# A new order table for a fused attention and maxout-FFN kernel: the same instructions, placed anew on the engines

## The chip, the cores and the metric

The kernel runs on one core of a Trainium2 chip. The metric is the device time of one execution in microseconds (us), as the median of several runs. A core has a tensor engine (PE, with its weight loads PEld), VectorE (DVE), ScalarE (ACT), GpSimd (POOL) and SyncE (SP). Each engine works through its own instructions strictly in order, and waits on semaphores for the others. Transfers between memory and the core are issued by SP (one DMA queue, q1 in the profile) or by POOL (another, q0) and are carried by 16 DMA engines, which both queues share.

## What is computed

```python
def phi(x):                       # x: [8, 8, 576, 64], w_phi: [64, 128]
    proj = einsum('bhsd,df->bhsf', x, w_phi)
    proj = proj - max(abs(proj), axis=-1, keepdims=True)
    return concatenate([exp(proj), exp(-proj)], axis=-1)
q_p, k_p = phi(q), phi(k)
kv  = einsum('bhsf,bhsd->bhfd', k_p, v)
num = einsum('bhsf,bhfd->bhsd', q_p, kv)
den = einsum('bhsf,bhf->bhs', q_p, sum(k_p, axis=2))[..., None] + 1e-06
x   = (num / den).transpose(0, 2, 1, 3).reshape(4608, 512)
h   = maximum(maximum(x @ w1, x @ w2), x @ w3)      # w1, w2, w3: [512, 768]
out = h @ w_out                                     # w_out: [768, 512]
```

Linear attention with a learned feature map, and behind it a feed-forward layer (FFN) that takes the maximum of three projections. All inputs and the output are 32-bit floats.

## The kernel before, in words

The attention is cut into 16 units (`attention(u)`, L429 on): unit u is half of the eight heads of batch u // 2, 18 tiles of 128 rows. A unit goes through these steps, each called a node:

- Loads. Units 0 to 3 have q and k loaded by POOL's queue, which turns them to bf16 on the way (L451, L466; k of unit 0 comes through SP, L458, and is cast, L462). Units 4 to 15 have them loaded by SP in 32 bits (`load`, L373 and L378) and cast by POOL (L510). The last 64 rows of each head of q, the tails, come in small pieces of 256 bytes through SP (L383), for two units at a time; units 0 to 3 have them cast by POOL (L487). v comes through SP (L373). For units 1 to 3 a one-element DVE copy (`gate`, L479) holds the load of v back until an earlier unit is transposed.
- Transposes of q and k: by PE (L495) with a DVE copy out (L500) for units 0 to 3, by a DMA transpose on SP (L514) for the others.
- Projections on PE (L536), two exponentials per group on ACT (L545), maxima of the absolute value on DVE (L548), the products of v with the exponential of the maxima (em, L558, on ACT) on POOL (`va`, L566).
- kv on PE (L587), the transposed projections and their exponentials (L607, L613), num and den on PE (L638), scaling, sum and quotient on DVE and POOL (L641, L644, L646, L648), and a transpose of the result into xT (PE L658, or a DMA on SP, L665).

The FFN uses max(x w1, x w2, x w3) = x w1 + max(0, x (w2 - w1), x (w3 - w1)). So w2 and w3 are replaced by their differences from w1 (L763): three pieces of w2 - w1 on POOL, three of w3 - w1 on DVE. The straight part x w1 w_out goes through a product of w1 and w_out that is computed once on the chip: w1 is transposed by PE (L775) and multiplied with w_out (L789). A chunk of 512 tokens (`chunk`, L671 on) takes for each of six columns an `up` group of four matmuls with w2 - w1 (L688), evacuated by ACT (L696) or DVE (L698), an `up2` group with w3 - w1 (L688 too), evacuated by DVE as a maximum (L694), then for each of four tiles the straight part (L716) and the down product (L721), an evacuation (L729) and a store through SP (L736). There are eight chunks, and a ninth for the tails of all batches, whose last tile is done in two halves of 256 columns: half i = 0 stores two pieces through SP, half i = 1 one through SP and one through ACT.

The four weights are loaded by POOL's queue, cast to bf16 on the way (L421): w1, w2 and w3 into w_bf, w_out into wout_bf.

What sets the order of it all is `PLAN`, a table of 1572 words made beforehand. A word such as `178S0@7.2` puts node 178 on SP (T is PE, D DVE, A ACT, G POOL, S SP), gives each of its buffers that is not placed yet a slot (0 here), and names a start time. `plan()` takes the nodes in the table's order, sets engine and slots, and emits them; each engine gets its instructions in that order. The start times serve only `fill()`, which may put idle matmuls into PE's gaps; it puts none here. The figures given with a node when it is built (costs, pipe, lat, packet, dmas) and the list of what it depends on are what a layout program would use. The replay doesn't read them. Waits follow from what the instructions read and write.

Of the kernel before, what the change touches and what calls it, by code (L numbers as in the profile page):

```python
# [89 lines left out]
401S0@12.2 44A0@12.2 98D@12.3 66A@12.4 46G0@12.5 69A@12.9 100D@13.0 108T112511@13.1 35A@13.2 38D@13.6 62A@13.6  # L90
113T31@13.8 256G@13.9 181G@14.1 70A@14.1 112D@14.2 45G@14.3 48A@14.4 103T40@14.6 109A@14.6 117D@14.8 257T2@14.9
104A@15.1 111D@15.4 261T3@15.6 61A@15.6 329S0@15.6 47G@15.7 49G@15.9 262D2@16.0 105A@16.1 107D@16.2 52T073@16.4
59A@16.5 106D@16.8 110A@17.0 50G@17.2 116D@17.4 60A@17.5 118T45@17.7 259T0@18.0 53A@18.0 122D@18.1 128A1@18.2
114A@18.4 123T67@18.5 51G@18.6 121D@18.7 400S@18.8 130G1@18.8 54A@18.9 152T411@18.9 115A@19.1 126D@19.4 154A@19.6
127D@19.7 55T31@19.7 124A@19.9 260D@20.0 119A@20.1 129G@20.1 182T6@20.4 56A@20.6 258D@20.7 125A@20.8 186T0@20.9
71A0@21.1 147T37@21.3 187D0@21.3 132A@21.3 57D@21.5 153A@21.5 72T20@21.6 135G@21.7 183D@21.7 120A@21.8 131G@21.9
75T14@22.0 133G@22.2 149A@22.3 73D0@22.3 184T5@22.4 76D@22.8 155A1@22.8 328S@22.9 151A@23.0 136T162@23.0 74D@23.2
148A@23.4 134G@23.5 77D@23.6 83T10@23.7 150A@23.9 138D@24.0 142T34@24.2 185D@24.2 137A@24.4 80T27@24.6 145A@24.6
78D0@24.8 139T65@25.0 84D1@25.1 143A@25.1 79G0@25.2 81D@25.5 146A@25.6 1187T1@25.7 85D@25.9 327S@26.0 144A@26.1
1185T2@26.3 82D@26.3 1188A0@26.6 406G1@26.6 141D@26.7 159T40@26.9 140D@27.0 86D1@27.2 156T37@27.2 160D0@27.5  # L100
1186A@27.5 87G@27.5 1183T5@27.6 157D@27.9 164T61@28.2 161D@28.3 1184A@28.5 223T4300@28.6 158D@28.7 88T2@28.9 404G@29.0
165D1@29.2 90T0@29.2 225A@29.4 403G@29.5 179D1@29.6 167T75@29.6 166D@29.7 1195T6@29.9 89A@29.9 405G@30.1 254D@30.1
168D@30.2 227A@30.5 162D0@30.7 334G2@30.7 91D@30.9 255S@31.0 224A@31.0 1189T21@31.2 163D1@31.4 226A@31.5 1196A@32.0
169D@32.1 1D@32.5 206T007000@32.6 197T4365@32.7 170D1@32.7 1190A@32.8 209D@33.0 172T1@33.3 171D@33.3 208A@33.5
1191T2@33.6 207A@33.9 201D@34.0 198A@34.2 180S@34.2 1179G@34.6 210D@34.7 199A@34.8 174T0@34.9 205D@35.0 1193T4@35.2
203A@35.3 200D@35.6 175A@35.8 173D@36.2 1192A@36.4 188T7630@36.6 1178G@36.7 1194A@36.9 228T1@37.0 1207T2@37.2
195D@37.3 230A@37.4 189A@37.7 196D@37.9 1209T4@38.1 229A@38.2 1208A1@38.4 204D@38.5 407G@38.8 1205T1@39.0 191D@39.1
202A@39.3 1177G@39.5 408S1@39.6 1181D@39.7 194A@39.7 1203T3@39.9 1210A@40.2 192D@40.3 1215T2@40.7 211A0@40.7
1182D@40.9 1204A@41.0 190A@41.5 1206D@41.5 331G@41.6 1217T5@41.6 193A@42.0 1216D@42.1 333G@42.2 272T11473611@42.6
212G0@42.7 1180D@42.8 218T10@43.0 277A@43.3 1219T2@43.3 280D@43.4 273A@43.8 276D@44.0 1221T3@44.2 222A@44.2 279D@44.6  # L110
219A@44.7 1201T4@45.1 1220D@45.2 274A@45.2 213G@45.2 220A@45.7 1218D@45.8 1213T2@45.9 1202A@46.2 1222D@46.4 278A@46.7
1199T1@46.8 275D@47.0 221A@47.2 1214D@47.6 214G@47.7 263T5436@47.8 332G@48.0 215T070@48.2 265A@48.5 271D@48.5
1200A@49.0 267D@49.1 281T23@49.4 268A@49.5 1211T1@49.6 285D@49.8 282A@50.0 270D@50.1 216A@50.2 1223T5@50.5 217A@50.6
1212D@50.8 231A0@50.9 269A@51.1 266D@51.4 243T27@51.4 544S0@51.7 240T01@51.7 284D@52.0 1224T@52.0 474S@52.3 244D0@52.3
286A1@52.5 283A@52.7 241D@52.8 287G1@52.8 335S0@52.9 264A@53.0 245D@53.2 235T62@53.3 242D@53.6 1225A0@53.6
293T3011@53.8 298T47@54.0 236D1@54.0 303T1@54.2 297A@54.2 1231T5@54.4 237D@54.6 304A@54.7 246D0@55.0 299A@55.0
232T62@55.3 288G@55.3 305A@55.5 1232T@55.6 301A@55.8 233D@55.9 300A@56.3 234D@56.4 302A@56.7 1227T1@56.9 238D1@57.0
296A@57.2 1233D1@57.2 294A@57.7 289G@57.8 247D0@57.9 409T00642700@57.9 480G0@58.1 290T105@58.3 295A@58.4 417D@58.6
479G@58.8 415A@58.8 412D@59.2 550G1@59.3 543S0@59.4 1228T@59.6 292A@59.8 416D@59.8 549G@60.0 473S@60.0 411A@60.1
291D@60.4 239G@60.6 306A1@60.6 475S@60.6 413D@60.8 414A@60.8 318T32@60.9 315T50@61.3 410A@61.3 319D0@61.5  # L120
366T7600@61.7 1229A2@61.8 545S0@61.9 316D@61.9 307T43@62.1 320D@62.4 369A@62.4 684S0@62.5 310T51@62.5 317D@62.8
368A@62.9 1235T2@62.9 547G@63.0 614S@63.1 308D1@63.2 370A@63.4 321D0@63.6 248T0@63.8 367A@63.8 311D@63.8 322G1@64.0
371T46@64.2 309D@64.3 249A@64.4 354T115711@64.5 330S1@64.5 1236T@64.7 312D@64.7 356A@65.0 313D1@65.3 374A@65.3
546G@65.4 314D@65.6 373A@65.7 325T3@66.0 478G@66.0 476S@66.0 375A@66.2 250T0@66.3 358D@66.4 323T1@66.6 477G@66.7
326D@66.7 251A@66.9 439T5611@67.0 324D@67.2 548G@67.2 441A@67.5 427T30@67.6 683S0@67.6 357D@67.7 690G2@67.7
1247T1@67.9 431D@68.0 355A@68.2 1237D3@68.4 440A@68.5 1241T3@68.7 372A@69.0 430D@69.0 615S@69.0 1248D0@69.3 442A@69.4
336T7524@69.7 428A@69.9 1239T1@70.2 429A@70.4 344D@70.4 1238S@70.6 443A@70.6 340D@71.0 1249T0@71.1 1242A@71.1
1226S@71.2 343D@71.6 1240A@71.6 402S@71.8 345T2673@72.1 339D@72.2 1250A@72.2 1245T1@72.6 347A@72.8 349D@72.8 613S@73.1
351A@73.3 348D@73.4 1261T0@73.5 687G@73.7 337A@73.8 352D@74.0 689G@74.3 1251T2@74.4 338A@74.4 1234S@74.6 353D@74.6
688G@74.8 359A0@74.9 346A@75.1 481S2@75.2 360G0@75.2 1253T5@75.2 1262D@75.3 1246A@75.6 1252D@75.9 362A@76.1  # L130
1259T7@76.1 342A@76.2 1254D@76.5 350A@76.7 418T6012@77.1 341A@77.2 376T3@77.5 361G@77.7 1243T5@77.7 425D@77.8
# [161 lines left out]
def kernel(  # L293
# [133 lines left out]
    def attention(u):  # L427
        un = units[u]
        b, ct0 = u // 2, (u % 2) * 2  # L429
        by_pe = u < BY_PE  # L430
# [15 lines left out]
        main_q, main_k, cast = [], [], {}  # L446
# [409 lines left out]
```

## Time and profile before

| | |
|---|---|
| median of 3 runs | 294.62 us (292.95 to 296.05) |
| the profiled execution | 292.23 us |
| its span, from the first instruction to the last | 290.1 us |
| PE busy | 270.6 us, 93% |
| DVE, ACT, POOL busy | 230.2, 204.7, 157.7 us |
| moved by DMA | 49.92 MB: q1 (SP) 44.25 MB, q0 (POOL) 5.08 MB |
| the four weight loads, from issue to landing | 14.2 us (w1), 20.0 (w_out), 25.1 (w2), 30.8 (w3) |

The profile is one execution. Busy time leaves out waiting. A row of a timeline has the start in us, the length in us, the engine, the line, the operation, what it writes and reads, and in brackets the engine's idle time ahead of it with what ended that. A row of the chain of waits has start, length, and the engine or transfer that held the chain for that long. In a row of the stretches the first field is the stretch, then its length, then each engine's busy time with its number of instructions, the granted clock of PE, the DMA share and the rate. A DMA queue's row has its packets, MB and the time its packets took as a share of 16 engines. An x behind a number counts instructions.

### The profile page before, as it was taken

What the parts mean: (1) busy time and instruction counts of PE and PEld (TensorE: products, weight loads), DVE (VectorE), ACT (ScalarE), POOL (GpSimd) and SP (SyncE); (2) the same over time, 40 slices, a digit from 0 to 9 for tenths busy, and PEclk for the clock granted to TensorE, in tenths of its full rate; (3) what the DMA queues carried; (4) which work ended last, traced back from release to release, by engine and by line L of the source; (5) the groups of instructions that cost most, each with busy time, mean ns of one, the idle gap of its engine ahead of it and who ended that gap; (6) DMA issues with size and microseconds to landing.
All of it is one profiled execution on the core that took longest, in us unless ns stands there. A gap on an engine that the chain in (4) does not pass through costs nothing.

```text
span 290.1 us, 8572 instructions
## 1 busy us (share of the span) xinstructions
PE 270.6 (93%) x3502; PEld 151.3 (52%) x3502; DVE 230.2 (79%) x458; ACT 204.7 (71%) x493; POOL 157.7 (54%) x163
## 2 busy tenths in 40 slices
PE   1589997899999999998999999999999999999994
PEld 1367643456546645663565445655465555444442
DVE  2699886989998889998999988999999785264430
ACT  2699985789998899689864899999969681210001
POOL 7397659557678636576866396660758533100000
PEclk9998999999999999999999999999999999999999
DMA  7999998793897962799987899627084212100065
GB/s 141 226 280 215 262 259 198 207 273 119 299 279 158 244 192 46 182 321 282 254 245 198 209 333 206 127 21 217 5 129 139 90 37 62 66 3 2 0 217 145
DMA packets 70662, 49.92 MB, mean 172 GB/s; under 512 B 47072, under 2 KB 58720, under 8 KB 70624
## 3 DMA queue, kind: packets, MB, share of 16 engines
q1 hardware_dynamic: 65232, 44.25, 58.7%
q0 software_dynamic: 5312, 5.08, 10.7%
q8 instruction: 27, 0.44, 0.6%
q14 instruction: 11, 0.09, 0.1%
q10 hardware_dynamic: 80, 0.07, 0.1%
HBM read 34.67 MB, written 9.44 MB: 152 GB/s over the span
## 4 chain that ended last, share of the span: by engine, by line
PE 74%; DMA 15%; DVE 6%; issue 1%; POOL 1%; SPq 1%; DVEq 0%; POOLq 0%
PE ups L688 31%; PE ops L721 14%; DMA w_bf<-in_moe_w_dram 11%; PE ops L716 10%; PE psn L638 6%; PE kvps L587 5%; PE psq L536 4%; PE psm L607 3%; DMA q_raw<-in_q_dram 2%; DMA xT<-x_sb 2%; DVE w_bf L763 1%; DVE x_sb L648 1%; DVE y L644 1%; PE pxT L658 1%; PE psk L536 1%
## 5 line engine op out<-in xcount | busy, mean ns | idle before, releaser
L688 PE MATMUL ups<-xT,w_bf 128*128 128x512 bf16 x432 | 99.5, 379 | 4.2 <-DVE w_bf L763 1.4
L545 ACT ACTIVATE Ek<-psk 128x512 bf16<-128x512 f32 (+1 forms) x160 | 83.6, 572 | 12.9 <-PE psk L536 6.7
L566 POOL TENSOR_TENSOR vab<-v_raw,em 128x1152 bf16<-128x1152 f32 (+1 forms) x36 | 69.5, 1950 | 35.8 <-ACT em L558 35.8
L613 ACT ACTIVATE Eq<-psm 128x512 bf16<-128x512 f32 (+1 forms) x160 | 81.9, 588 | 3.1 <-PE psm L607 1.9
L688 PEld LDWEIGHTS <-w_bf 128*128 128x128 bf16 x432 | 39.9, 98 | 52.6 <-issue 4.4
L548 DVE TENSOR_REDUCE mk<-psk 128x4 f32<-128x512 f32 (+1 forms) x80 | 48.7, 630 | 4.7 <-PE psk L536 3.2
L721 PE MATMUL ops<-wout_bf,hT 128*128 128x512 bf16 (+1 forms) x222 | 51.7, 373 | 0.0
L548 DVE TENSOR_REDUCE mq<-psq 128x4 f32<-128x512 f32 (+1 forms) x80 | 48.6, 628 | 2.3 <-PE psk L536 1.3
L696 ACT ACTIVATE hT<-ups 128x512 bf16<-128x512 f32 x36 | 21.8, 611 | 29.0 <-PE ups L688 28.8
L694 DVE TENSOR_TENSOR hT<-hT,ups 128x512 bf16<-128x512 bf16 x54 | 35.2, 678 | 8.3 <-PE ups L688 7.5
L648 POOL TENSOR_TENSOR x_sb<-y,rden 128x640 bf16<-128x640 f32 x22 | 27.4, 1253 | 21.9 <-DVE rden L646 21.0
L641 DVE TENSOR_TENSOR y<-psn,sq 128x325 f32<-128x325 f32 x64 | 29.5, 488 | 6.9 <-PE psn L638 5.0
L721 PEld LDWEIGHTS <-hT 128*128 128x128 bf16 x222 | 20.5, 98 | 21.9 <-issue 0.5
L644 DVE TENSOR_TENSOR y<-y,psn 128x325 f32<-128x325 f32 x64 | 29.4, 488 | 1.4
L638 PEld LDWEIGHTS <-Eq 128*128 128x128 bf16 x640 | 25.0, 97 | 10.3 <-issue 2.5
L729 ACT COPY osb<-ops 128x512 f32<-128x512 f32 (+1 forms) x23 | 13.2, 583 | 23.0 <-PE ops L721 22.7
L638 PE MATMUL psn<-kv_sb,Eq 128*128 128x65 bf16 x640 | 27.5, 194 | 1.3 <-issue 0.4
L536 PE MATMUL psq<-wph,qkT 64*128 64x128 bf16 x288 | 25.9, 224 | 1.2 <-DVE qkT L500 1.0
L536 PEld LDWEIGHTS <-qkT 64*128 64x128 bf16 x576 | 18.6, 97 | 15.8 <-issue 12.0
L536 PE MATMUL psk<-wph,qkT 64*128 64x128 bf16 x288 | 25.4, 224 | 0.3 <-DVE v_raw L479 0.3
L716 PE MATMUL ops<-xT 128*128 128x512 bf16 x96 | 24.6, 380 | 0.0
L587 PE MATMUL kvps<-vab,Ek 64*128 64x65 bf16 x1152 | 22.7, 193 | 0.3 <-ACT Eq L613 0.2
(58 smaller groups left out, 259.9 us busy)
## 6 DMA issues: line engine op xcount, KB each, us to landing
v_raw<-in_v_dram SPq DMA_DIRECT2D x16, 576.0 KB, 7.2
out_dram<-osb SPq DMA_DIRECT2D x32, 256.0 KB, 3.4
k_raw<-in_k_dram SPq DMA_DIRECT2D x12, 576.0 KB, 5.4
q_raw<-in_q_dram SPq DMA_DIRECT2D x12, 512.0 KB, 5.5
w_bf<-in_moe_w_dram POOLq DMA_DIRECT2D x3, 768.0 KB, 25.1
q_raw<-in_q_dram SPq DMA_DIRECT2D x16, 64.0 KB, 5.5
qk_bf<-in_k_dram POOLq DMA_DIRECT2D x3, 288.0 KB, 7.3
qk_bf<-in_q_dram POOLq DMA_DIRECT2D x3, 256.0 KB, 9.9
```

The costliest lines, as they stand in the source:

```text
L536: nc.tensor.matmul(ps()[:, i, :], lhsT=cols[r0:r0 + D, :], rhs=wph[r0:r0 + D, :], start=True, stop=True)
L545: "ek", {"ACT": 0.485 if n == 4 else 0.28}, lambda s=s, t0=t0, n=n, psk=psk: nc.scalar.activation(Ek[s]()[:, t0:t0 + n, :], psk()[:, 0:n, ...
L548: reds.append(nd(kind, {"DVE": 0.607 if n == 4 else 0.34}, lambda ps=ps, m=m, t0=t0, n=n: nc.vector.tensor_reduce(m()[:, t0:t0 + n], ps()[ ...
L566: made.append(any_of(n_, lambda n_, g=g, t0=t0, t1=t1: (nc.vector if n_.eng == "DVE" else nc.gpsimd).tensor_tensor(vab()[:, g, t0:t1, 0:D] ...
L587: nc.tensor.matmul(kvps[ab]()[:, pr, g, :], lhsT=Ek[g]()[r, t, :], rhs=vab()[r, g, t, :], start=(pr == prs[0] and g + j == 0), stop=(pr == ...
L613: "eq", {"ACT": 0.485 if n == 4 else 0.28}, lambda s=s, t0=t0, n=n, psm=psm: nc.scalar.activation(Eq[s]()[:, t0 * P:(t0 + n) * P], psm()[: ...
L638: nc.tensor.matmul(psn[g]()[:, c, :], lhsT=Eq[g]()[:, t0:t0 + P], rhs=kv()[:, pr, ab, g, :], start=True, stop=True)
L644: sums.append(nd("xw", {"DVE": 0.42}, lambda ab=ab, psn=psn, y=y: nc.vector.tensor_tensor(y()[:, ab], y()[:, ab], psn[1](), ALU.add), [n_] ...
L688: nc.tensor.matmul(ups(), lhsT=w_bf[i + 1][:, ct, j * P:(j + 1) * P], rhs=tokens_of(ct), start=(ct == 0), stop=(ct == CT - 1))
L694: nc.vector.tensor_tensor(hT()[:, j, :], hT()[:, j, :], ups(), ALU.max)
L716: nc.tensor.matmul(ops_()[:, 0:width], lhsT=tile_of(ct, tt), rhs=line_w[c_i > MOVE][:, ct, cols], start=(ct == 0), stop=False)
L721: nc.tensor.matmul(ops_()[:, 0:width], lhsT=hT()[:, j, tt * P:(tt + 1) * P], rhs=wout_bf[:, j, cols], start=False, stop=(j == JT - 1))
```

## The change

PLAN is replaced by another table of the same 1572 nodes. Two lines of node descriptions change with it:

```diff
-                           pipe=0.6, hold=-2.0, lat=2.5 if by_pe else 1.7, dmas=2, packet=18.0)
+                           pipe=1.44, lat=1.7, dmas=2, packet=45.0)
...
-                need = [tail, main_k[-1]] if i == 2 else [main_q[-1], main_k[-1]] if i else [main_q[0], main_k[0]]
+                need = [tail, main_k[-1]] if i == 2 else [main_q[-1]] + main_k if i else [main_q[0], main_k[0]]
```

The first are figures for the tail loads, the second says that the second batch of transposes of a unit needs both halves of k. The new table has one text line fewer, so that later lines have numbers lower by one in the changed kernel; this document uses the numbers of the kernel before.

No instruction is added or removed, and each node keeps its shape. Nodes that may run on two engines are in part dealt anew. The first lines of the tables:

```diff
-4G0@0.4 6S0@0.4 2S@1.0 0G@1.2 5G@1.8 8S@2.2 93G1@2.7 10S0@2.8 92G@3.5 7D@3.7 11S0@4.1 3D@4.2 13T0@4.3 253G2@4.3
-14D0@5.0 252G@5.2 9A@5.3 24T001200@5.8 19T34@6.0 27D@6.3 21A@6.5 12G@6.6 15T5@6.7 96G@6.8 23D@6.9 26A@7.0 17T6@7.2
...
+1508T@269.9 1517D2@270.1 1540D@270.7 1518S@270.9 1503T5@271.2 1513D3@271.4 1509D0@272.0 1504T@272.0 1544D@272.6
```

What the new order says, read by node (k3 is the load of k for unit 3, and so on):

- POOL's loads. Before: q0 first half, q0 second half, k1, q1, k3, q3, casts of the tails of units 0 and 1, k2, q2, w1, w_out, w2, w3, then unit 0's products. After: q0 second half, q0 first half, q1, k1, k2, q2, w1, casts of the tails, q3, k3, w_out, unit 0's products (with the casts of the tails of units 2 and 3), w2, unit 1's four products, two x of unit 0 (L648), w3, and the three differences w2 - w1.
- SP's loads. Before: k0 first half, w_phi, k0 second half, tails of 0 and 1, v0, tails of 2 and 3, v1, k5, tails of 4 and 5, q5, k4, q4, v3, v2, transpose of unit 5. After: k0 second half, k0 first half, w_phi, tails of 0 and 1, v0, tails of 2 and 3, v1, k5, q5, v2, k4, q4, tails of 4 and 5, v3, transpose of unit 5.
- PE. Unit 0's second batch is transposed ahead of its first, and unit 2's transposes stand ahead of unit 3's. Ahead of the first up group both orders have the same matmuls, but for one of psm (256 columns) that the new one has more.
- DVE. Before, the three differences w3 - w1 stand behind four maxima: difference, maximum, difference, the first evacuation of an up group (L698), its up2 (L694), difference. After: the first evacuation, four maxima, difference, evacuation, two maxima, difference, difference, and only then the first up2.
- POOL behind the differences w2 - w1. Before, a cast of unit 5 stands ahead of the last difference, and two casts of unit 4, then unit 2's products. After: four casts of unit 5, unit 2's two products, the last cast of unit 5 and four casts of unit 4, unit 3's products.
- The end. The last half tile is i = 1 before, and i = 0 after.

More of the change, by code (lines that the diff above doesn't have):

```diff
@@ L90 @@
[L90 to L99, printed above, removed]
@@ L240 @@
[L240 to L243 removed]
+8S0@0.7 5G0@1.2 6S@1.3 2S@1.9 0G@2.1 4G@2.6 10S0@3.1 92G1@3.5 9A@3.9 93G@4.3 11S0@4.4 177G2@5.2 7D@5.4 3D@5.9 176G@6.0
+15T0@6.0 13T1@6.7 16D0@6.7 1173G@6.8 14D@7.4 34T000200@7.5 29T34@7.7 36A@8.0 38D@8.0 24T51@8.1 19T67@8.4 31A@8.4
@@ new lines @@
+1359T5@160.1 785A1@160.4 838A@160.6 1364D0@160.6 786G1@160.7 1367T6@160.9 788A@161.1 1360A@161.2 1366D@161.2
+837A@161.7 1346S@161.9 841T2710@161.9 1368A@162.2 792T4511@162.4 849D@162.6 1361T3@162.7 795A@162.8 787G@163.2
+848D@163.2 793A@163.3 1377T1@163.6 844D@163.8 794A@164.0 1371T6@164.4 845D@164.4 855A0@164.6 843A@164.8 1362D@165.0
+796A@165.3 1373T2@165.3 1372D@165.7 858G0@165.7 842A@165.8 1106G1@166.0 846A@166.2 802T3@166.3 1378D@166.3
+797T54@166.4 857G@166.5 789T067@166.6 805A0@166.7 971S2@166.9 1374D@166.9 801A@166.9 847A@167.4 867T2100@167.8
@@ L244 @@
+1569D0@280.3 1564T@280.5 1571A@280.8 1570S@281.2 1565A2@281.4 1566S@281.9
 """
```

296 lines of the change are left out of this document (149 added, 147 removed).

## The prediction

> **What bounds the kernel now.** I read the page's busy rows first, then busy time cut into stretches, then the chain of waits where the tensor engine (PE) idles, then the DMA queues in those places.
>
> ```profile
> span 290.1 us, 8572 instructions
> PE 270.6 (93%) x3502; PEld 151.3 (52%) x3502; DVE 230.2 (79%) x458; ACT 204.7 (71%) x493; POOL 157.7 (54%) x163
> ```
>
> PE is busy for 270.6 of 290.1 us. No PE instruction is added or removed, so what can change is its 19.5 us of idle time. The stretches show where that lies (the first number is the stretch's length, the second PE's busy time):
>
> ```profile
> core 0: us, PE busy (x) PEld busy (x) DVE busy (x) ACT busy (x) POOL busy (x), PEclk, DMA share, GB/s
> 0.00:34.70 34.70, 24.03 (x485) 18.15 (x486) 24.98 (x57) 25.92 (x63) 24.91 (x40) 0.95 1.08 224
> 34.70:42.70 8.00, 7.38 (x78) 3.84 (x74) 6.70 (x16) 7.13 (x16) 2.94 (x3) 1.00 1.13 254
> 42.70:54.00 11.30, 8.64 (x52) 3.63 (x53) 8.78 (x14) 7.46 (x17) 11.30 (x8) 1.00 0.89 245
> 54.00:286.20 232.20, 230.53 (x2895) 125.67 (x2893) 189.30 (x373) 164.15 (x399) 118.56 (x115) 1.00 0.63 159
> 286.20:290.10 3.90, 0.00 (x0) 0.00 (x0) 0.42 (x1) 0.00 (x0) 0.00 (x0) 1.00 0.36 115
> ```
>
> From 54 us to its last matmul PE idles 1.67 us, and 3.9 us at the end. The rest is ahead of 54 us: 10.67, 0.62 and 2.66 us. In those first 54 us the DMA share is 0.9 to 1.1, and these rows tell what PE waited for (the chain's pieces: start, length, what; then timeline rows of GpSimd (POOL), PE and POOL):
>
> ```profile
> 16.17 30.79 DMA w_bf<-in_moe_w_dram
> ...
> 47.05 1.05 DVE w_bf L763
> 48.11 0.60 DVE mq L548
> 48.71 0.55 DVE w_bf L763
> ...
> 50.87 1.33 DVE w_bf L763
> 52.20 0.61 DVE mq L548
> ...
> 52.85 3.68 PE ups L688 x16
> ...
> 57.08 1.15 PE kvps L587 x72
> ...
> 59.32 0.86 PE ops L716 x4
> 60.18 0.62 PE psn L638 x20
> 60.80 1.29 PE ops L721 x6
> ```
> ```profile
> 13.88 0.76 POOL L421 DMA_DIRECT2D w_bf<-in_moe_w_dram  x1
> ...
> 31.49 1.25 POOL L648 TENSOR_TENSOR x_sb<-y,rden 128x640 bf16<-128x640 f32 x1 [0.28 <-DVE rden L646]
> ...
> 40.62 4.20 POOL L763 TENSOR_TENSOR w_bf<-w_bf 128x1024 bf16<-128x1024 bf16 x2 [3.42 <-DMA w_bf<-in_moe_w_dram]
> ...
> 45.43 2.12 POOL L763 TENSOR_TENSOR w_bf<-w_bf 128x1024 bf16<-128x1024 bf16 x1
> ...
> 48.52 0.61 POOL L510 CAST qk_bf<-k_raw 128x512 bf16<-128x512 f32 x1
> 49.10 5.08 POOL L566 TENSOR_TENSOR vab<-v_raw,em 128x1152 bf16<-128x1152 f32 x2
> ```
> ```profile
> 42.79 0.39 PE L688 MATMUL ups<-xT,w_bf 128*128 128x512 bf16 x1 [0.71 <-POOL w_bf L763]
> ```
>
> The first FFN matmul starts at 42.79 because w2 lands at about 40.5 and POOL then needs 2.1 us for the first difference w2-w1. The next wait is w3: issued at 16.17, landed at 46.96. VectorE (DVE) needs it for three differences, stands still for it with its other work behind it, and so PE loses 2.66 us. From 54 us on the kernel runs at PE's pace.
>
> **The change, part by part.** Only the table of order, engines and slots acts. The altered costs (pipe, lat, packet) and the list "need" feed a layout that has already been made; the replay takes from the table the order on each engine, the engine and the slot. I use the order alone and none of its times.
>
> *1. The weights in the POOL queue (q0).* Before: q0, k1, q1, k3, q3, k2, q2, w1, w_out, w2, w3. After: q0, q1, k1, k2, q2, w1, q3, k3, w_out, w2, w3. Up to w2's end q0 moves the same transfers; only what shares the engines with it differs. These rows of the DMA view (2 or 4 us each: 24:26, 28:32, 36:40, 42:44; packets, MB, share) price it:
>
> ```profile
> q0 software_dynamic: 247, 0.33, 91.8%
> q1 hardware_dynamic: 255, 0.06, 23.8%
> ```
> ```profile
> q0 software_dynamic: 467, 0.48, 70.4%
> q1 hardware_dynamic: 466, 0.54, 46.2%
> ```
> ```profile
> q0 software_dynamic: 375, 0.55, 76.1%
> q1 hardware_dynamic: 376, 0.38, 35.2%
> ```
> ```profile
> q0 software_dynamic: 147, 0.22, 60.0%
> q1 hardware_dynamic: 164, 0.35, 50.6%
> ```
>
> While both queues have work they send nearly equal counts, whatever a packet's size: they take turns. With 16 engines a turn costs: weight (1536 B) with 256 B, 2 x 16 / 247 = 130 ns; w_out (1024 B) with 1024 B, 4 x 16 / 467 = 137 ns; weight with 1024 B, 171 ns; weight with 2304 B (k or v), 218 ns. So w_out with 2304 B is about 137 + 47 = 184 ns, an estimate.
>
> Now w2's landing in the new order. The first q0, k1, q1 and a further k and q are ahead in both; in the old order that sixth transfer was issued at 5.63 and took 11.1 us:
>
> ```profile
> 5.63 0.79 POOL L451 DMA_DIRECT2D qk_bf<-in_q_dram  x1
> ```
> ```profile
> qk_bf<-in_q_dram POOLq DMA_DIRECT2D x1, 256.0 KB, 11.1
> ```
>
> So w1 starts at 16.7. Its 32 packets per engine take turns with v1 and k5: 32 x 218 ns, to 23.7. q3 (32) goes beside the q load of unit 5: under the 137 ns row, say 100, to 26.9. k3 (16) is about alone: 90, to 28.3. w_out (48): some 11 alone at 90, then SP's v2 and k4 (32 turns at 184) and 5 at 137: to 35.9. w2: 27 turns with q4 at 171, 5 with the tails at 130: to 41.2. That is 0.7 us later than before: **+0.7**. Bounds: were no load of SP's there after 28.3, w_out at 137 - 41 = 96 and w2 at 130 give 37.1 (-3.4); were all of them 2304 B, 48 x 184 + 32 x 218 give 44.1 (+3.6). PE's work ahead of the first up (L688) is the same but for one 256-wide psm matmul, and the wait covers it: 0. That unit 0's second half of q and k is turned first is covered by the same wait.
>
> A rule of the Trainium skill bears on this: DMA: Bandwidth & Descriptors, section "Queues, rings and completion order", says that each engine goes round robin over the queues but drains a whole packet, some 9 to 17 descriptors, from one before it switches. The trace agrees on the equal counts (467 and 466); how many descriptors one turn holds it does not show. By the rule w2 could end earlier or later by one such stay on the other queue, at 35.2% x 4 us x 16 / 376 = 60 ns each some 0.5 to 1.0 us, an estimate; the sum below would then be off by as much.
>
> *2. w3's wait.* After w2, w3 shares turns with the rest of SP's tails (27 x 130) and v3 (5 x 218): landed at 45.8. In DVE's new order the first w3 difference stands behind the first evacuation (L698) and four maxima that follow it; DVE gets there at 43.5 + 0.9 for the first four up matmuls + 5 x 0.6 = 47.4, so the 2.66 us stall goes. What is late next are the second and third difference, back to back at 1.05 and 1.33 us, against the third and fifth up2 matmul group; I leave 0.4 us for that: **-2.3**. Bounds: all of it (-2.7), nothing (0). In the new POOL order w3's issue stands behind unit 1's four products and both x of unit 0; that costs nothing as long as POOL gets there before w2 has landed at 41.2. The old order had that x done at 32.7 (31.49 + 1.25). The issues themselves (0.76 us each, the first POOL row) now delay unit 1's products and the differences; PE's wait for w_out and w2 covers that.
>
> *3. The order from 54 us on.* PE idles only 1.67 us there. The order differs everywhere and no row prices it; it can win those 1.7 us or lose as much again, and I take 0. Other moves of q_raw, k_raw and v_raw loads on SP stand ahead of work that is some 10 us later; hidden.
>
> *4. The end.* Before, the last piece's two stores left from SP and ACT side by side:
>
> ```profile
> 286.21 0.42 DVE L729 COPY osb<-ops 128x256 f32<-128x256 f32 x1 [3.21 <-PE ops L721]
> 286.67 0.56 ACTq L736 DMA_DIRECT2D out_dram<-osb  x1
> ```
>
> After, the last half is i = 0, whose two stores are both SP's: one more issue of 0.56 us in a row, less what ACT's shorter copy gains: **+0.4** (0 to +0.6).
>
> Sum: +0.7 - 2.3 + 0 + 0.4 = -1.2 us: span 288.9. The profiled execution took 292.23 us for its span of 290.1, and 2.39 us less than the median of 294.62 (292.95 to 296.05). Against that median the forecast is **293.4 us**, -0.4%.
>
> **The rivals.**
>
> *A: the weights come earlier than priced.* If SP's loads of units 2 and 4 come late (v2 waits on DVE for its gate copy), w_out and w2 run alone: up to -3.4 instead of +0.7, and w3's wait is gone. -3.4 - 2.3 + 0.4 = -5.3: 289.3 us. For it: before, the rows from 24 to 44 us show q1 with work in each turn; now SP's queue pauses between units 5 and 2. Against it: the same bytes have still to pass before unit 4.
>
> *B: the change does nothing.* w2 and w3 land up to 3.6 us later and the stall is only moved: +3.6 - 2.3 + 0.4, +1.7: 296.3 us. For it: POOL's queue carries the same bytes up to w2's end. Against it: it needs 2304-byte packets in all 80 turns, and SP's queue has them for 32.
>
> *C: slower, by unit 5's transpose.* POOL's new order puts the three differences, four casts and unit 2's two products ahead of the last cast that unit 5's transpose on SP (L514) waits for. w2 41.2 + 3 x 2.12 + 4 x 0.6 + 5.08 + 0.3 = 55.3; the transpose then takes 5.3 us:
>
> ```profile
> qkT<-qk_bf SPq DMA_TRANSPOSE x1, 5.3
> ```
>
> It lands at 60.6; PE gets to unit 5's projection (L536), behind 12 groups of four L688 matmuls (0.9 each), three L716 of 0.86, two L721 of 1.29, 1.24 of psn, 1.15 of kvps and some 2 us of projections, 20 us in all after 43.5 and the 0.4 of step 2, at about 63.8. So 3.2 us are spare; each later us goes on the time. What could use them up is this wait of POOL's:
>
> ```profile
> POOL vab L566 <- ACT em L558: 35.8, 11, 10.4
> ```
>
> If unit 2's products wait 10.4 us for em, PE loses 7.2: -1.2 + 7.2 = +6.0: 300.6 us. From 7.3 us of such waiting on it is over 1% slower. Against it: unit 2's projections stand ahead of the first up, so em should be there some 5 us before POOL is.
>
> **How the numbers follow.** A measurement of this kernel can tell about 1% (2.9 us) from no change. Forecast 0.48, A 0.25, B 0.12, C 0.15. Faster by over 1% (below 291.7): A, and 0.04 of the forecast's low end, 0.29. Slower by over 1% (above 297.6): C and 0.03 of B, 0.18. Within: 0.53. The likeliest case alone covers 291.5 to 295.5 (w2 1.5 us either way, and 0.5 for the later stages). The range runs from A's 289.3 to 297.0, above B, and leaves out C and a little beyond A.
>
> **What would show it.** Step 1: POOL's first L763 starts at 41 to 42, the first L688 at 43 to 44; rival A has them before 40. Step 2: DVE's first L763 no longer waits for DMA, and PE's idle time in the 11 us behind the first up is below 1 us. Step 3: PE idle under 2 us from there to its last matmul. Step 4: the stretch behind the last matmul is 4.1 to 4.5 us. C would show as PE L536 waiting for DMA qkT at 60 to 70 us. A first L688 outside 40 to 46, or over 3 us of PE idle time behind it, makes the prediction wrong.

## The result and the profile after

| | before | after |
|---|---|---|
| median | 293.01 us (291.40 to 296.31, 17 runs) | 291.29 us (290.02 to 292.32, 17 runs) |
| the profiled execution | 292.23 us, span 290.1 | 291.29 us, span 289.5 |

The ratio is 0.9939, with a 95% interval of 0.9913 to 0.9966: 0.6% faster, less than the 1% named as the smallest difference to be told from none. The forecast was 293.4 us, or 0.4% less. The 17 runs of before include the three from which the prediction started; its median came down by 1.6 us with the other 14, which is most of the 2.1 us by which the absolute time lies below the forecast, and the only reason why 291.29 lies under the 291.7 named as "faster by over 1%". Every ratio leaves out runs over 1.5% above the fastest of their kernel, few in most cases but 2 of 8 and 7 of 12 in two experiments further down (the differences ahead of the products, and all moves), whose traces are of executions 4 to 6 us above their lowest and are read for the places of waits alone.

Line numbers of the changed kernel and of all experiments on it are one lower than before's: L687 is the up group, L693 the evacuation of up2, L697 that of up, L762 the differences of the weights, L565 POOL's products, L647 the x, L735 the store.

The page of after, first part:

```profile
span 289.5 us, 8537 instructions
...
PE 268.4 (93%) x3461; PEld 151.7 (52%) x3502; DVE 236.1 (82%) x466; ACT 199.7 (69%) x486; POOL 157.1 (54%) x162
```

41 matmul records are missing in this trace (3461 against 3502 weight loads), so PE's busy sum is some microseconds short and isn't compared with before's 270.6. The stretches, with the bounds used before, the last two cut at PE's last matmul:

```profile
0.00:34.70 34.70, 24.46 (x478) 18.58 (x479) 25.92 (x59) 25.79 (x66) 22.58 (x34) 0.95 1.11 224
34.70:42.70 8.00, 7.43 (x68) 3.79 (x70) 6.69 (x15) 6.53 (x16) 4.84 (x3) 1.00 1.11 273
42.70:54.00 11.30, 9.71 (x73) 4.25 (x72) 10.91 (x16) 10.59 (x27) 10.05 (x10) 1.00 0.26 78
54.00:285.12 231.12, 226.81 (x2848) 125.12 (x2884) 192.54 (x379) 156.41 (x380) 119.67 (x118) 1.00 0.68 167
285.12:289.50 4.38, 0.00 (x0) 0.00 (x0) 0.00 (x0) 0.37 (x1) 0.00 (x0) 0.74 0.44 104
```

The timelines of PE, DVE and POOL in after:

```profile
35.96 2.77 PE L788 MATMUL pm<-wout_bf,hT 128*128 128x512 bf16 x11
...
43.13 0.39 PE L687 MATMUL ups<-xT,w_bf 128*128 128x512 bf16 x1
...
53.86 2.81 PE L687 MATMUL ups<-xT,w_bf 128*128 128x512 bf16 x12 [1.49 <-DVE w_bf L762]
```
```profile
39.71 1.02 DVE L647 TENSOR_TENSOR x_sb<-y,rden 128x640 bf16<-128x640 f32 x1
...
48.07 0.68 DVE L762 TENSOR_TENSOR w_bf<-w_bf 128x1024 bf16<-128x1024 bf16 x1
...
50.10 3.70 DVE L762 TENSOR_TENSOR w_bf<-w_bf 128x1024 bf16<-128x1024 bf16 x2
```
```profile
20.45 0.29 POOL L486 CAST qk_bf<-q_raw 128x128 bf16<-128x128 f32 x1 [3.57 <-DMA q_raw<-in_q_dram]
...
37.85 6.94 POOL L762 TENSOR_TENSOR w_bf<-w_bf 128x1024 bf16<-128x1024 bf16 x3 [5.22 <-DMA w_bf<-in_moe_w_dram]
...
48.38 4.87 POOL L565 TENSOR_TENSOR vab<-v_raw,em 128x1152 bf16<-128x1152 f32 x2 [1.25 <-ACT em L557]
```

Cut at two marks, the first up group and PE's last matmul, the span comes apart in three terms:

| | before | after | measured | predicted |
|---|---|---|---|---|
| first up group starts | 42.79 | 43.13 | +0.34 | +0.7 |
| from there to PE's last matmul | 243.39 | 241.98 | -1.41 | -2.3 |
| from there to the end | 3.91 | 4.40 | +0.49 | +0.4 |
| sum | | | -0.58 | -1.2 |

The total is near, but two of the terms come about in another way than forecast. w2 landed at 37.8 (POOL's row at 37.85), not at 41.2, and yet PE began no earlier: 43.13 is over 5 us behind the landing, and some 3 us behind the end of POOL's first difference at 40.0. And DVE's first difference at 48.07 waits for nothing, as forecast (w3 landed at 44.4), yet PE then waits 1.49 us for the third: its two last differences take 3.70 us.

### The profile page after: what moved, and what is told of

The parts are those of the page before. It is cut to its first block, busy times and chain, and to the rows that moved or that the text cites. A ratio compares the mean times of both kernels' runs of the same rounds, so it can differ in the third digit from the quotient of the medians.

```text
span 289.5 us, 8537 instructions
## 1 busy us (share of the span) xinstructions
PE 268.4 (93%) x3461; PEld 151.7 (52%) x3502; DVE 236.1 (82%) x466; ACT 199.7 (69%) x486; POOL 157.1 (54%) x162
## 4 chain that ended last, share of the span: by engine, by line
PE 76%; ACT 5%; DVE 4%; issue 3%; DMA 2%; POOL 1%; SPq 0%; ACTq 0%; DVEq 0%
PE ups L687 30%; PE ops L720 13%; PE ops L715 9%; PE psn L637 7%; PE kvps L586 5%; PE psq L535 4%; ACT Eq L612 4%; PE psm L606 3%; PE pm L788 2%; DMA xT<-x_sb 2%; DVE hT L693 1%; PE psk L535 1%; ACT Ek L544 1%; DVE mk L547 1%; DMA out_dram<-osb 1%
## 5 line engine op out<-in xcount | busy, mean ns | idle before, releaser
L687 PE MATMUL ups<-xT,w_bf 128*128 128x512 bf16 x413 | 98.3, 379 | 2.7 <-DVE w_bf L762 1.5
L565 POOL TENSOR_TENSOR vab<-v_raw,em 128x1152 bf16<-128x1152 f32 (+1 forms) x36 | 68.6, 1927 | 37.2 <-ACT em L557 33.4
L687 PEld LDWEIGHTS <-w_bf 128*128 128x128 bf16 x432 | 39.8, 98 | 49.2 <-DVE w_bf L762 2.4
L720 PE MATMUL ops<-wout_bf,hT 128*128 128x512 bf16 (+1 forms) x217 | 50.7, 373 | 0.3 <-issue 0.2
L647 POOL TENSOR_TENSOR x_sb<-y,rden 128x640 bf16<-128x640 f32 x22 | 28.1, 1285 | 21.4 <-DVE rden L645 19.4
L693 DVE TENSOR_TENSOR hT<-hT,ups 128x512 bf16<-128x512 bf16 x54 | 35.8, 681 | 4.5 <-PE ups L687 3.9
L637 PEld LDWEIGHTS <-Eq 128*128 128x128 bf16 x640 | 26.0, 99 | 11.9 <-issue 3.4
L720 PEld LDWEIGHTS <-hT 128*128 128x128 bf16 x222 | 20.4, 98 | 21.5 <-issue 0.3
L637 PE MATMUL psn<-kv_sb,Eq 128*128 128x65 bf16 x640 | 28.3, 196 | 1.7 <-DVE y L640 0.8
L695 ACT ACTIVATE hT<-ups 128x512 bf16<-128x512 f32 x31 | 18.3, 620 | 14.2 <-PE ups L687 13.9
L697 DVE TENSOR_SCALAR hT<-ups 128x512 bf16<-128x512 f32 x23 | 15.7, 686 | 14.1 <-PE ups L687 14.0
L715 PE MATMUL ops<-xT 128*128 128x512 bf16 x82 | 23.8, 380 | 1.2 <-DVE mk L547 0.3
```

The lines of the kernel that those rows point to most:

```text
L565: made.append(any_of(n_, lambda n_, g=g, t0=t0, t1=t1: (nc.vector if n_.eng == "DVE" else nc.gpsimd).tensor_tensor(vab()[:, g, t0:t1, 0:D] ...
L637: nc.tensor.matmul(psn[g]()[:, c, :], lhsT=Eq[g]()[:, t0:t0 + P], rhs=kv()[:, pr, ab, g, :], start=True, stop=True)
L687: nc.tensor.matmul(ups(), lhsT=w_bf[i + 1][:, ct, j * P:(j + 1) * P], rhs=tokens_of(ct), start=(ct == 0), stop=(ct == CT - 1))
L693: nc.vector.tensor_tensor(hT()[:, j, :], hT()[:, j, :], ups(), ALU.max)
L715: nc.tensor.matmul(ops_()[:, 0:width], lhsT=tile_of(ct, tt), rhs=line_w[c_i > MOVE][:, ct, cols], start=(ct == 0), stop=False)
L720: nc.tensor.matmul(ops_()[:, 0:width], lhsT=hT()[:, j, tt * P:(tt + 1) * P], rhs=wout_bf[:, j, cols], start=False, stop=(j == JT - 1))
```

## The theories

*Theory 1, the tails.* The casts of the tails of units 2 and 3 now wait 3.57 us (POOL's row at 20.45), with unit 0's last two products behind them. The two queues in after from 16 to 18 us:

```profile
q0 software_dynamic: 220, 0.34, 92.1%
q1 hardware_dynamic: 223, 0.07, 23.5%
```

Equal counts again: a tail packet of 256 bytes costs a turn of a 1536-byte packet of w1, which the new order puts there. The second tail landed at 20.39, and at 17.18 before. That would hold PE up by the 1.2 us by which its products of w_out begin later (35.96 against 34.75). The rival: PE is late for another reason.

*Theory 2, a blocked DVE.* A DVE operation with two operands in SBUF (the on-chip memory that the engines work from) stands still while POOL works on SBUF. All durations of the three equal differences in after:

```profile
L762 POOL TENSOR_TENSOR w_bf<-w_bf x3: 2124/2190/2692, 37.9 to 42.7; 128x1024 bf16<-128x1024 bf16 x3
L762 DVE TENSOR_TENSOR w_bf<-w_bf x3: 681/1175/2601, 48.1 to 51.2; 128x1024 bf16<-128x1024 bf16 x3
```

The row has the shortest, the median and the longest in ns. 0.68 us was the one at 48.07, begun while POOL waited for em; 1.17 and 2.60 those beside the two products at 48.38. The rival: they are long, or late, on their own account.

## The experiments

All are the changed kernel with some words of its table moved, so that an engine's order changes and nothing else; each ratio is to runs of the kernel before beside it.

**The tails' casts behind unit 0's products (POOL).**

```diff
-cast of a tail, cast of em, cast of a tail, va of unit 0 x2
+cast of em, va of unit 0 x2, cast of a tail x2
```

> Edit of the changed kernel: on POOL the casts of the tails of units 2 and 3 stand behind unit 0's four products instead of between them (and SP's q load of unit 5 behind the casts). Theory 1, the tails hold up unit 0: the products of unit 0's second half start at 16 to 18 us instead of 21.1, PE loses 1 to 2 us less by 27 us, the first up (L687) starts at 41 to 42.3 instead of 43.2, and the time falls by about 1 us, to 0.990 of the kernel before. Rival, the recorded step 1 (w_out and w2 set the pace): the first up stays at 43.2 and the time at 0.994.

291.95 us, ratio 0.9953 (0.9925 to 0.9981). POOL and PE:

```profile
16.93 2.26 POOL L565 TENSOR_TENSOR vab<-v_raw,em 128x576 bf16<-128x576 f32 x2
20.38 0.53 POOL L486 CAST qk_bf<-q_raw 128x128 bf16<-128x128 f32 x2 [1.19 <-DMA q_raw<-in_q_dram]
```
```profile
42.58 1.90 PE L687 MATMUL ups<-xT,w_bf 128*128 128x512 bf16 x8 [0.49 <-POOL w_bf L762]
...
52.17 1.04 PE L687 MATMUL ups<-xT,w_bf 128*128 128x512 bf16 x4 [1.17 <-DVE w_bf L762]
54.69 2.81 PE L687 MATMUL ups<-xT,w_bf 128*128 128x512 bf16 x12 [1.49 <-DVE w_bf L762]
```

The products are 4.2 us earlier and PE's products of w_out 1.1 us (34.86). But SP's loads came earlier too (v of unit 2 issued at 27.9, and 29.1 in after) and took turns with w_out and w2, which landed at 40.3: the first up at 42.58 now waits for w2. And two of DVE's differences took 2.47 and 2.60 us, so PE waits twice. What was won was given back; the 0.990 of theory 1 was not reached. Whether the 1.1 us were the tails' is taken up below.

**w1 behind unit 3's q and k (POOL's queue).**

```diff
-w1, cast of a tail x2, q3, k3, w_out
+cast of a tail x2, q3, k3, w1, w_out
```

> Edit of the changed kernel: w1 is issued behind q3 and k3 instead of ahead of them, nothing else. Theory 1, the 256-byte tails of units 2 and 3 take turns with w1's packets: with q3's 512-byte packets beside them instead they land at 17 to 18 us instead of 20.4, and unit 0's second products start at 17 to 18.5; w1 lands at 26 to 28 instead of 22.5, so that its transposes on PE (L774) wait for it, and the first up comes within 0.7 us of 43.2. Rival, the tails are late for their own sake (their later issue, or the HBM): they stay at 20 to 21.

292.38 us, ratio 0.9989 (0.9951 to 1.0027). PE:

```profile
27.82 1.90 PE L774 MATMUL pwT<-ident,w_bf 128*128 128x128 bf16 x24 [2.06 <-DMA w_bf<-in_moe_w_dram]
...
46.16 1.90 PE L687 MATMUL ups<-xT,w_bf 128*128 128x512 bf16 x8
```

The tails landed at 15.86 and 16.48, so it is w1's packets that they wait for. But w1 came at 27.8, PE waited for it, and the first up is 3 us later than in after, where 0.7 us had been expected at most. In this execution, then, w1's early place, which brought the tails' delay, is worth more than it costs; the two ratios' intervals overlap, so the times don't show it. (The trace is of a run of 294.20 us, 1.8 above the median.)

**All three DVE differences as early as w3 allows.**

```diff
-evacuation, max x4, difference, evacuation, max x2, difference x2, up2
+evacuation, difference x3, max x4, evacuation, max x2, up2
```

> Edit of the changed kernel: DVE's three differences w3 - w1 stand directly behind its first evacuation of an up group, ahead of four maxima, not behind them. Theory 2, DVE's differences are held up by POOL's products of unit 2, which start at 48.4 (0.68 us beside an idle POOL, 2.60 us beside a product): at 45.8 to 48.5 they take 0.7 to 1.2 us each, PE's stall of 1.5 us at 53 us goes, PE idles under 0.5 us between 49 and 55, and the time falls by 1 to 1.4 us, to 0.989. Rival 1, the third difference is long whatever stands beside it: one still takes over 2 us. Rival 2, the maxima that are now later hold up unit 3, and a wait of 1 us or more comes back in another place: 0.994.

293.96 us, ratio 1.0024 (0.9981 to 1.0067). The differences and PE:

```profile
L762 DVE TENSOR_TENSOR w_bf<-w_bf x3: 1091/1197/1442, 44.8 to 47.3; 128x1024 bf16<-128x1024 bf16 x3
```
```profile
49.60 3.50 PE L687 MATMUL ups<-xT,w_bf 128*128 128x512 bf16 x8 [3.20 <-DVE mq L547]
```

Away from the products none takes over 1.5 us. But the maxima behind them give back the PSUM (the memory that PE writes its results to; its eight banks go round among all kinds of products here) that the next up groups need: PE waits for the maxima instead, which was the second rival named.

**The last half tile.** Its order is put so that one of the last stores leaves through ACT again.

```diff
-ACT: store, copy of 256 columns
+ACT: copy of 256 columns, store
```

> Edit of the changed kernel: the last half tile is i = 1 again, whose two stores leave from SP and ACT. Recorded step 4: the stretch from PE's last matmul to the end shortens by 0.4 to 0.6 us, and the time falls by as much, to 0.992 or 0.993. Rival: the last landing sets the end whatever issues it, no difference (0.994).

291.54 us, ratio 0.9949 (0.9916 to 0.9982); 4.22 us from the last matmul to the end, against 4.40. Only 0.18 us in the trace, where 0.4 to 0.6 were expected, and nothing in the time; that two stores of the other half still stand ahead in SP's queue would account for it, but was not tested.

**The kernel before, once more.**

> The kernel before once more, for a second profile of it. If the first profile stands for its usual execution: first up at 42.8, the differences of DVE at 47 to 52 us, 2.5 to 2.8 us of idle PE between 42.7 and 54 us, a span of 290 to 291. If its times above 293 us have a cause in the first 54 us, a longer one shows there by the same amount as in the span.

292.17 us, span 290.0, first up at 42.65, PE's last matmul at 286.1, differences on DVE of 0.82, 1.04 and 1.41 us: the first profile is repeated. It doesn't show what the runs of before above 293 us are made of.

**The third difference on POOL.**

```diff
-POOL: va of unit 2 x2, cast x5; DVE: ... difference x2, up2
+POOL: cast x5, difference, va of unit 2 x2; DVE: ... difference, up2
```

> Edit of the changed kernel: the casts for unit 4 and unit 5's last one, and the third difference w3 - w1 (taken from DVE), stand on POOL ahead of unit 2's products. Theory 2, DVE's two-operand differences are blocked by POOL's products: the two that DVE keeps run beside casts and take 0.7 to 1.3 us, the third takes 2.1 to 2.7 us on POOL and is done by 52.5, PE's wait of 1.5 us at 52 to 54 goes, and the time falls by 1.0 to 1.6 us, to 0.989. Rival, DVE is late for its own work: PE's wait stays over 1 us, or comes back as unit 2's products, now 4 us later, make kv of unit 2 (L586) wait at 57; 0.994.

292.06 us, ratio 0.9953 (0.9932 to 0.9975). The differences on DVE, and PE:

```profile
L762 DVE TENSOR_TENSOR w_bf<-w_bf x2: 675/804/932, 47.0 to 49.1; 128x1024 bf16<-128x1024 bf16 x2
```
```profile
42.06 1.90 PE L687 MATMUL ups<-xT,w_bf 128*128 128x512 bf16 x8 [0.16 <-POOL w_bf L762]
...
54.28 4.10 PE L687 MATMUL ups<-xT,w_bf 128*128 128x512 bf16 x12 [2.95 <-POOL w_bf L762]
```

With no product beside them DVE's differences take 0.93 and 0.68 us, as theory 2 has it. POOL however finishes its own only at 54.2, and PE waits 2.95 us. The first up is at 42.06 with the order ahead of it that after has: the 43.13 of after isn't the order's alone.

**Tails behind, and the gate of unit 2 later on DVE,** so that SP's loads don't come earlier.

```diff
-DVE: gate of unit 2, copy of w1's transpose, kv copy x3
+DVE: copy of w1's transpose, kv copy x3, gate of unit 2
```

> e1 and one more edit: the gate copy that lets v2 and the loads behind it on SP go stands 2 us later on DVE. Theory 3, in e1 those loads came 1.2 us earlier (SP at 27.9 instead of 29.1) and took turns with w_out and w2, which then landed at 33.8 and 40.3 instead of 31.7 and 37.8: with SP at 29.3 to 30.5 w_out lands at 31 to 32.3, w2 at 37 to 38.7, and the first up comes at 41.5 to 42.2 instead of 42.6. DVE's differences still meet POOL's products, so the time is 0.992 to 0.996. Rival, w2's landing in e1 has another cause: it stays over 39.5.

290.56 us, ratio 0.9913 (0.9882 to 0.9944). w2 landed at 38.2, and PE's products of w_out start at 34.79. Yet the first up is at 43.39. DVE and PE:

```profile
38.54 2.56 DVE L647 TENSOR_TENSOR x_sb<-y,rden 128x640 bf16<-128x640 f32 x1
```
```profile
41.16 0.45 PE L657 MATMUL pxT<-ident,x_sb 128*128 128x128 bf16 x5 [1.26 <-DVE x_sb L647]
...
43.39 0.39 PE L687 MATMUL ups<-xT,w_bf 128*128 128x512 bf16 x1
```

This x has two operands in SBUF. It takes 0.81 us in the trace of the third difference on POOL, where w2 lands at 39.8, behind it; 2.56 here, where POOL began its differences at 38.30. So w2 early makes POOL start early, and POOL then blocks the x that PE needs: theory 2 at a second place. The trace of the last half tile, which has after's order up to there, repeats it: POOL starts at 38.10, the x takes 2.04 us, and PE waits 0.74 us for it.

**These moves together** (tails, gate, third difference on POOL, last half tile).

> e9, e8 and e5 together: tails' casts behind unit 0's products, the later gate, the third difference on POOL ahead of unit 2's products, the last half i = 1. If the three theories hold and add up: first up at 41.5 to 42.2, no wait of PE over 0.5 us from there to 57 us, a stretch of 4.2 us at the end, and the time 2.0 to 3.0 us below the changed kernel, 0.984 to 0.988 of the kernel before. Rival, the gains only move the wait on (to w3, to unit 2's kv, or to a place behind 60 us): 0.990 or more.

291.11 us, ratio 0.9932 (0.99 to 0.9964). First up at 42.26, but PE waits over 2 us for POOL's difference, as with that move alone.

**The differences ahead of the products.** POOL does five casts ahead of unit 2's products, and DVE its two last differences ahead of two maxima.

```diff
-POOL: va of unit 2 x2, cast x5; DVE: max x2, difference x2
+POOL: cast x5, va of unit 2 x2; DVE: difference x2, max x2
```

> The changed kernel with two moves: POOL does the last cast of unit 5 and the four casts of unit 4 ahead of unit 2's two products, not behind them, and DVE does its second and third difference (L762) ahead of two maxima of unit 3, not behind them. So all three differences of DVE should fall beside casts and not beside products. Theory 2 (a DVE difference of two SBUF operands stands still while POOL multiplies, which is what left PE 1.5 us to wait): the three take 0.7 to 1.2 us each, the third ends at about 51, the row of L687 at 53 to 54 loses its wait, PE idles under 0.5 us between 46 and 54 us, and the time is 1.0 to 1.5 us below that of the changed kernel, some 290.0 us; unit 2's products end at about 55.5 and are in time. Rival theory (the 2.60 us belong to the operation or to its place, or what is won is lost again because unit 2's products come 2 us later): a difference of over 2 us stays, or PE waits as long for kvps of unit 2 or for a maximum; the time is that of the changed kernel within 0.4 us.

289.89 us, ratio 0.9877 (0.9836 to 0.9918). The trace is of a run of 294.89: DVE, PE, and the stretch behind.

```profile
50.15 3.68 DVE L762 TENSOR_TENSOR w_bf<-w_bf 128x1024 bf16<-128x1024 bf16 x2
```
```profile
54.55 6.18 PE L687 MATMUL ups<-xT,w_bf 128*128 128x512 bf16 x20 [3.25 <-DVE mq L547]
```
```profile
50.00:58.00 8.00, 4.48 (x14) 1.57 (x14) 5.96 (x8) 4.21 (x12) 5.80 (x4) 0.81 0.87 164
```

In this execution the product began at 50.72, before the third difference, which was blocked after all, and with the two maxima behind it PE stood still for 3.25 us. Its clock (the column ahead of the DMA share) was then 0.81 over these 8 us. So the trace shows one way in which a long run comes about. That the short ones keep clear of the product is only argued; none of them was profiled.

**The control: only DVE's order changed.**

```diff
-DVE: max x2, difference x2
+DVE: difference x2, max x2
```

> The control to the run beside it: only DVE's second and third difference are moved ahead of the two maxima of unit 3; POOL's order is that of the changed kernel, with unit 2's two products at 48.4 to 53.3. Theory 2 (the product holds DVE's difference up): the differences begin 0.7 us earlier, at 49.4, and one or both of them still take over 2 us; the third ends at 53 or later, PE's wait of 1.5 us stays within 0.5 us, and the time is that of the changed kernel within 0.4 us. Rival theory (the differences only begin too late): both take about 1.2 us, the third ends at about 51.8, PE's wait is gone and the time falls by about 1.4 us.

293.53 us, ratio 1.0042 (1.0006 to 1.0079). DVE and PE:

```profile
49.19 3.57 DVE L762 TENSOR_TENSOR w_bf<-w_bf 128x1024 bf16<-128x1024 bf16 x2
```
```profile
53.49 4.49 PE L687 MATMUL ups<-xT,w_bf 128*128 128x512 bf16 x20 [3.14 <-DVE mq L547]
```

A start 0.9 us earlier shortens the pair by 0.13 us only (3.57 against 3.70), since the products (49.66 to 54.7) are still beside it: the third still takes 2.60 us. The rival "they only begin too late" falls, as it wanted both at about 1.2 us. The time is not that of after: PE waits 3.14 us, for the maxima that now stand behind the blocked operations. That was missed.

**All moves that helped.**

> All moves that helped, together: the casts of the tails of units 2 and 3 behind unit 0's products, unit 2's gate and the loads of SP behind it earlier on DVE, DVE's differences and POOL's casts as in the run with the differences ahead of the products, and the last half tile with one of its stores on ACT. If the moves act in different places of the span, as their traces have it (weights, differences, tail), the gains add: the first L687 at 42.5 to 43.4, no wait of over 0.5 us for a difference, 4.2 us behind the last matmul, and 290.56 less 1.4 less 0.2, some 289 us. If they use up the same slack, the time is that of the version with tails and gate, 290.6 us within 0.5 us, and another wait (w3 or kvps of unit 2) shows in place of the one that went.

Median 294.40 us; four of its runs took 289.3 to 290.7 us and eight 293.3 to 296.2, ratio 0.9906 (0.9853 to 0.996). The trace (293.33) has the first up at 42.39 and the same 3.24 us of waiting for a maximum. The gains don't add. It would fit that the order with the maxima behind depends on which of two operations starts first; only one of the eight long runs was profiled, and none of the four short ones.

**The second product behind the casts.** The version with tails and gate, DVE's order untouched; between unit 2's two products POOL does four casts.

```diff
-POOL: va of unit 2 x2, cast x4, cast
+POOL: va of unit 2, cast x4, va of unit 2, cast
```

> The version with tails and gate (290.56 us) with one move more: POOL does the last cast of unit 5 and three casts of unit 4 between the two products of unit 2, not behind both. DVE's order is unchanged, so the maxima of unit 3 stay where they are and the third difference falls beside casts. Theory 2 (a product of POOL holds a DVE difference up): the first two differences take 0.7 and some 1.2 us as before, the third 0.7 to 1.2 in place of 2.60 and ends at about 52.5; PE's wait of 1.5 us ahead of the up group at 54 us goes; unit 2's second product ends at about 56 and is just in time; the time is 1.0 to 1.5 us lower, some 289.3 us. Rival theory (what is won is lost again, as in the runs with the moved differences: another wait of the same chain takes its place, here kvps of unit 2 behind the later product, or the evacuations of DVE that are still to come): a wait of over 1 us shows in PE between 50 and 60 us, and the time is 290.6 us within 0.5.

289.56 us (288.35 to 289.94), ratio 0.9883 (0.9843 to 0.9922), the lowest median, with none of its six runs out of line. DVE, POOL and PE:

```profile
47.64 0.94 DVE L762 TENSOR_TENSOR w_bf<-w_bf 128x1024 bf16<-128x1024 bf16 x1
...
49.77 3.17 DVE L762 TENSOR_TENSOR w_bf<-w_bf 128x1024 bf16<-128x1024 bf16 x2
```
```profile
49.58 2.12 POOL L565 TENSOR_TENSOR vab<-v_raw,em 128x1152 bf16<-128x1152 f32 x1
51.64 1.76 POOL L509 CAST qk_bf<-q_raw 128x128 bf16<-128x128 f32 x2
```
```profile
52.30 3.63 PE L687 MATMUL ups<-xT,w_bf 128*128 128x512 bf16 x16 [1.17 <-DVE w_bf L762]
```

The second difference began 0.2 us behind the product, took 2.47 us, and ended at 52.24, some 0.5 us behind the product's end at 51.70. The third, beside a cast, took 0.77. So the length follows from what POOL does beside the operation, whichever of the three it is. The wait did not go, though, as was expected: it is 1.17 us and not 1.49. In this execution w2 landed 2.3 us later than in the version with tails and gate (40.5 against 38.2), POOL was later with it, and the first product met the second difference. Both have the same order up to there and v of unit 2 issued at 29.62 and 29.89, so the gate's place does not fix w2's landing by itself; what does is open. Against that version the intervals overlap, so that the 1.0 us between them is not shown; the span of the two traces differs by 1.4 us, 0.7 of it ahead of the first up.

## Why the prediction came out as it did

*Step 1 (+0.7; measured +0.34): the size near by luck, the reasons wrong.* The failing statements are that SP's v2 and k4 stand beside w_out, which put w2's landing at 41.2, and that PE's work ahead of the first up costs nothing because the wait for w2 covers it. SP:

```profile
21.14 0.37 SPq L377 DMA_DIRECT2D q_raw<-in_q_dram  x1
29.12 0.37 SPq L372 DMA_DIRECT2D v_raw<-in_v_dram  x1
```

Between these issues lie 8 us, since v2 waits on its gate on DVE. In that time w_out ran partly alone: it landed at 31.7, not at 35.9, which is more than the whole miss, and w2 at 37.8. (The 90 ns of the sum for a packet of a queue alone stand on no row of before; in after, from 30 to 32 us, with 330 packets of q0 against 3 of q1, a packet took 2 x 16 / 330 = 97 ns.) That is rival A's mechanism, and within its figures. But the price of a transfer isn't the price of its wait: with w2 off the path PE's own work came last, and that cover was gone.

What made PE late? Theory 1 alone does not account for it. These stretches of PE have the same order in them, after first, then the kernel with all differences early:

```profile
20.00:30.00 10.00, 8.41 (x217) 6.95 (x213) 8.63 (x22) 8.27 (x25) 8.99 (x11) 0.83 1.18 260
```
```profile
20.00:30.00 10.00, 8.86 (x248) 7.49 (x245) 8.82 (x24) 8.80 (x26) 9.50 (x12) 1.00 1.18 263
```

In both the second tail landed within 0.05 us of 20.4. With a clock of 1.00 the products of w_out start at 34.95 and the first up at 42.12; with 0.83, at 35.96 and 43.13. So a microsecond of it goes with the granted clock in that execution, and what counts is when the clock is low. In after it is low late:

```profile
24.00:26.00 2.00, 1.75 (x26) 1.31 (x25) 1.13 (x4) 2.00 (x9) 1.99 (x3) 0.60 1.19 233
26.00:28.00 2.00, 2.00 (x29) 1.63 (x28) 1.95 (x7) 1.68 (x5) 2.00 (x3) 0.55 1.16 242
```

The one other trace with a low clock from 24 to 28 us (0.54, the differences ahead of the products) has the products of w_out at 36.23. In all others but the one with w1 moved the clock is 0.98 or more there, and they start at 34.44 to 35.19, also where it was 0.58 to 0.62 from 20 to 24 us (34.79 with tails and gate, 34.74 with the second product behind; in before 34.75, and 34.78 with a full clock once more). With the clock full from 24 us on, the tails' place makes little difference: where the tails landed at 19.2 and at 18.8 (third difference on POOL; control) the start is 34.66 and 34.44, some 0.3 to 0.5 us sooner than with 20.4, and the 4 us that the first experiment gave unit 0's products brought 0.1 us (34.86). No trace has the tails behind and a low clock from 24 to 28 us, so whether the tails took away the slack that would have covered it stays open.

So 43.13 is one execution's. Six traces have after's order up to the first up, and it starts at 42.06 to 43.52 in them: at 42.06 and 42.12 with next to nothing in the way (third difference on POOL; all differences early), some 0.7 us sooner than before; at 43.13 and 43.52 with the low clock; at 43.19 with the blocked x (last half tile); at 42.80 where w2 landed at 40.6 (control). In after itself the x is hardly blocked, 1.02 us against 0.81, and PE does not wait for it.

*Step 2 (-2.3; measured -1.41): the mechanism right, the size off.* The wait for w3 went. What was left was put at 0.4 us, from 1.05 and 1.33 us for two differences in before (its first and third; its second took 1.04); they took 1.17 and 2.60, because the new order puts unit 2's products beside them. PE idles 1.59 us from 42.7 to 54, where before idled 2.66, and not below 1; the rest of the -1.41, some 0.3 to 0.4 us, lies behind 54 us and isn't traced. That before's rows already held this lock (1.33 beside a product) was not seen: the term was priced by durations of the old neighbourhood.

*Step 3 (0): right within its bounds.* From 54 us on the waits of PE that the traces name come to 1.5 us before and about 2 us after, none over 0.9 us; the lost records don't allow a closer sum of idle time.

*Step 4 (+0.4; measured +0.49): right in size.* The experiment on it won 0.18 back in its trace, so two stores in one queue are shown as part of it only.

*The rivals.* A's early transfers came, its 5.3 us did not, because PE's own work ahead of the first up took their place. B was wrong: no stall was moved to a later w3. C was not seen: unit 2's products waited 1.25 us for em, not 7.3.

*What stays open.* The medians differ by 1.7 us, the profiled executions by 0.9, the spans by 0.6. Before ranges to 296.3 us, after only to 292.3; no trace of a long run of before was had. Since the first up moves by over a microsecond between executions of one order, one profile against one can't settle a difference of this size.

## What to carry to other kernels

When a transfer is moved off the path, look for what waits next, and for what it starts: here early weights set POOL to work beside a DVE operation that PE needed. Durations hold for the neighbours they were measured with; before moving an operation with two SBUF operands, look at what the other engine does at its new place. And an order in which an operation keeps clear of another by 0.5 us may give two kinds of runs, as the two experiments with maxima behind the differences suggest; put the gap where the table leaves a microsecond.

## What the runs showed of the hardware

- DVE against POOL. The difference of 128x1024 took 0.68 us where POOL was idle when it began, 0.68 to 1.2 beside casts, 1.17 and 1.41 beside a product that was ending (after, before), 2.47 and 2.60 beside one that had begun at most 0.5 us earlier; the x of 128x640 0.81 alone, 1.02 to 2.56 beside POOL's differences. POOL loses as well: one of its differences took 2.69 instead of 2.12, and a product up to 2.56. In the profile such an operation is a long row and not idle time, so a table of waits doesn't name POOL. The Trainium skill states this in "SBUF — State Buffer", section "Who interferes with whom": a DVE instruction with two SBUF inputs contends with a GpSimd instruction that reads SBUF, and the one that comes second is blocked for the whole of the other. The traces agree: the blocked difference ended 0.54 us behind the product's end at 51.70 (second product behind), and 0.55 behind it in before (52.20 against 51.65) and in after (51.28 against 50.73).
- The clock behind a stall. In the stretch from 50 to 58 us the granted clock was 0.79 to 0.85 in five of the six traces in which PE had stood still for more than 2 us in a row (0.81 in the row above); the control's 3.14 us left it at 1.00. In the traces quoted with waits of 1.5 us and less there it was 1.00. So such a stall costs more than itself, by chance: 0.15 to 0.21 of 8 us is 1.2 to 1.7 us of PE's pace, an estimate. The Trainium skill, "TensorE: Matmul & The Clock Gate", Part 1, has the clock fall after an idle window of about 3.4 us that runs freely. The chance agrees with that, the length does not: the stalls behind which it fell here were of 2.40 to 3.25 us, all shorter than that window. The 0.83 from 20 to 30 us in after, where no wait is longer than 0.7 us, does not follow from it either.
- A 256-byte packet pays for its neighbour: the second tail landed 3.2 us later than in before (20.39 against 17.18) with w1's packets beside it, at nearly equal counts (220 and 223), and at 16.48 with w1 moved behind.
